# Table seeds by VectorE in 32-bit words, and nine more up products through ScalarE, in a fused S4 convolution and gated GLU

## The chip, the cores and the metric

The kernel runs on one core of a Trainium2 chip. The time is that of one execution in device microseconds; a kernel's time is the median of its runs. The engines are TensorE (PE in the profile, with PEld for its weight loads), VectorE (DVE), ScalarE (ACT), GpSimd (POOL) and SyncE (SP), which here issues most of the DMAs.

## The reference

The input u has 2048 tokens of 512 features. It is layer-normed to xn, and the output is a sum of three terms:

```python
xn = _layernorm(x, axis=-1)
return x + _A_ref(xn, A_re, A_im, B_re, B_im, C_re, C_im, log_dt, Dskip) + _B_ref(xn, w_gate, w_up, w_down)

# _A_ref: a convolution along the tokens, one kernel K per feature, from 128 complex modes
logdA = dt * A ; dB = dt * Bc
P = jnp.exp(logdA[:, :, None] * l[None, None, :])        # l = 0 .. 2047
K = jnp.einsum("dn,dnl,dn->dl", Cc, P, dB).real
y = irfft(rfft(K padded) * rfft(xn padded))[:L] + xn * Dskip
# _B_ref
h = _sigmoid(x @ w_gate) * (x @ w_up)                    # 512 -> 1792
return h @ w_down                                        # 1792 -> 512
```

In the reference the lags l are cast to bfloat16, so that lags above 256 fall on a coarser grid.

## The kernel before, in words

Two jobs share the engines. The GLU goes in four groups of 512 tokens. For each of the 14 tiles of 128 hidden features TensorE computes a gate product (L1045) and an up product (L1069) into PSUM, ScalarE applies the sigmoid to the gate (L1057, or L1060 for two at once), and VectorE multiplies. For the tiles in `UEV` ScalarE first copies the up product from PSUM to a buffer `us_sb` (L1084); two neighbours share a buffer of 2 x 512, and VectorE multiplies both at once on SBUF alone (L1089). The other tiles are multiplied straight from PSUM (L1094). The down products (L1123) follow.

The convolution goes by a transform over blocks of tokens. Its kernel K is built from tables, in four chunks c of 128 features. A ladder of squarings gives the powers W[k] with exponent 2^k (L669 to L678, cast at L661 and L663). From W the kernel builds G (16 lags) and H (41 lags, `LAG0`), each laid out with 64 pairs of features outermost, then real or imaginary, then the lag, then the two features of a pair. H is seeded with eight lags that are entries of W: the copies at L775 to L777, run by ScalarE, or by VectorE for the operation numbers in `ON_DVE` (L288 and L286 in the profile, with the other copies of the helper). The other lags come from complex products (`powers`, L737 to L743) and from squares (`squares`, ScalarE at L791, VectorE at L796 and L797). When a chunk's tables are done, TensorE multiplies G and H (L822, two halves of 64 matmuls for each chunk), ScalarE evicts the results to `kq_sb`, two DMAs store them to `k_scr` (L833, 96 KB each), and a DMA per chunk brings them back in another layout (L837, 192 KB). Two chunks make a half p of the features. A short VectorE operation adds the skip term (L844), and only then the transformed kernel of that half can be computed (L911), evicted, multiplied with the transformed input (L916 and L920), and transformed back (L935). Eight units of work u per half do this. The half swaps that L916 needs are DMAs (L893) or, for five units of the second half, VectorE copies (L898). The results go through memory once more and are summed with the GLU in the tail (L994, L1020, L1143).

The order of work is written out by hand. `_Plan.add` numbers the operations as they are created, `ORDER` lists all the numbers, and `run` issues them in that order; each engine keeps the order of its own operations. The costs, priorities and due times handed to `add` (`PSIG`, `PPROD` and so on) thus have no part in the order of issue. Buffers are pools of slots, taken and given back in the order of the list. To find what stands ahead of what on an engine, one counts off the creations and looks the numbers up in `ORDER`. Some of the numbers for c = 3 and the half that it ends:

| operation | number before | number after |
|---|---|---|
| first and last seed copy | 337 to 344 | 321 to 323 |
| last part of the last powers (L742, L743) | 366 | 345 |
| last part of G | 335 | 319 |
| G times H, first half (L822) | 367 | 346 |
| stores to k_scr | 371, 372 | 350, 351 |
| reload of the half | 277 and 373 in parts | 352 |
| skip term (L844) | 374 | 353 |

Of the kernel before, what the change touches and what calls it, by code (L numbers as in the profile page):

```python
# [10 lines left out]
BF = mybir.dt.bfloat16  # L11
# [14 lines left out]
FT = 14  # L26
# [3 lines left out]
CW = 128  # L30
# [17 lines left out]
FLIP = ((0, 3), (0, 5), (1, 0), (1, 1), (1, 2), (1, 4), (1, 5), (1, 6), (2, 0), (2, 4), (3, 2))  # L48
# [13 lines left out]
LAG0 = [0, 1, 3, 5, 7, 6, 4, 2, 8, 10, 14, 12, 9, 11, 13, 15, 256, 262, 260, 258, 264, 266, 270, 268, 524, 520, 516, 512, 780, 776, 772, 768,  # L62
        1024, 1032, 1544, 1536, 1280, 1288, 1800, 1792, 2048]
EXP = {5: 1, 9: 1, 10: 1, 11: 3, 17: 1, 21: 1, 22: 1, 23: 3, 24: 3, 25: 1, 26: 1, 28: 3, 29: 1, 30: 1, 33: 3, 34: 3, 35: 1, 37: 3, 38: 3, 39: 1}
# [118 lines left out]
def _consts():  # L183
# [19 lines left out]
UEV = (6, 7, 10, 11, 12, 13, 14, 15, 16, 17, 18, 19, 22, 23, 24, 25, 26, 27, 28, 29, 30, 31, 32, 33, 34, 35, 36, 37, 38, 39, 40, 41, 44, 45, 46, 47, 52, 53, 54, 55,)  # L203
ON_DVE = (86, 89, 104, 106, 121, 122, 123, 137, 138, 184, 194, 195, 198, 199, 201,)
ON_ACT = (2,)
ORDER = [
# [112 lines left out]
def kernel(  # L319
# [61 lines left out]
    def at(off, shape, dt=BF):  # L381
# [141 lines left out]
    for n in (0, 5, 6):  # L523
        keep_warm(3 if n < 3 else 1, -9 + n)
# [688 lines left out]
```

## Time and profile before

| | |
|---|---|
| median of 3 runs | 215.45 us (214.41 to 215.57) |
| the profiled execution | 215.32 us, of which its span 213.4 us |
| mean granted TensorE clock | 0.997 |
| PE busy | 204.0 us |
| DVE busy | 191.3 us |
| ACT busy | 176.3 us |
| POOL busy | 33.1 us |
| DMA, mean over the span | 200 GB/s |

The span runs from the first to the last instruction of the profiled execution; its times are measured from its start. In the groups of instructions a line gives the line of the kernel, engine and operation, the output and input by name and form, the count, then the busy time and the mean ns of one, then the idle time of the engine ahead of them. Instructions on one engine overlap a little at their ends, so that the distance from start to start is shorter than the duration. In the rows of busy time by stretch the engines stand in the order PE, PEld, DVE, ACT, POOL, with the granted clock, the share of the DMA engines and GB/s behind them. In a row of waits stand the total in us, the number of waits and the longest.

### The profile page before, as it was taken

What the parts mean: (1) busy time and instruction counts of PE and PEld (TensorE: products, weight loads), DVE (VectorE), ACT (ScalarE), POOL (GpSimd) and SP (SyncE); (2) the same over time, 40 slices, a digit from 0 to 9 for tenths busy, and PEclk for the clock granted to TensorE, in tenths of its full rate; (3) what the DMA queues carried; (4) which work ended last, traced back from release to release, by engine and by line L of the source; (5) the groups of instructions that cost most, each with busy time, mean ns of one, the idle gap of its engine ahead of it and who ended that gap; (6) DMA issues with size and microseconds to landing.
All of it is one profiled execution on the core that took longest, in us unless ns stands there. A gap on an engine that the chain in (4) does not pass through costs nothing.

```text
span 213.4 us, 4897 instructions
## 1 busy us (share of the span) xinstructions
PE 204.0 (96%) x1839; PEld 103.2 (48%) x1864; DVE 191.3 (90%) x406; ACT 176.3 (83%) x284; POOL 33.1 (15%) x40
## 2 busy tenths in 40 slices
PE   7989999999999999999999999999999999999892
PEld 2654444444444454345447464444644655644472
DVE  4799999999999999999999999999973999990494
ACT  4799999999999999998998999779979699960000
POOL 2108030003040000010009970011200000000000
PEclk9999999999999999999999999999999999999998
DMA  5998597013963218788776369589994789897955
GB/s 148 330 372 313 182 225 237 2 52 133 260 139 60 98 55 263 185 238 212 215 216 159 112 174 275 141 231 244 175 257 112 203 252 335 246 288 209 263 195 178
DMA packets 52377, 42.61 MB, mean 200 GB/s; under 512 B 16641, under 2 KB 44546, under 8 KB 52354
## 3 DMA queue, kind: packets, MB, share of 16 engines
q1 hardware_dynamic: 50658, 40.30, 64.3%
q0 software_dynamic: 864, 1.57, 4.8%
q10 hardware_dynamic: 832, 0.43, 0.8%
q8 instruction: 14, 0.23, 0.4%
q14 instruction: 9, 0.07, 0.1%
HBM read 24.99 MB, written 12.85 MB: 177 GB/s over the span
## 4 chain that ended last, share of the span: by engine, by line
PE 59%; ACT 20%; DMA 9%; DVE 6%; issue 4%; POOL 1%; DVEq 0%; ACTq 0%; SPq 0%
PE bank L1069 15%; PE bank L1123 13%; PE bank L1045 11%; PE pair L911 9%; ACT big L288 6%; PE pair L935 5%; ACT hT_sb L1057 3%; PE pair L1045 3%; DMA k_scr<-kq_sb 3%; ACT us_sb L1084 3%; ACT big L669 3%; ACT big L663 2%; DVE big L1020 2%; DMA big<-v_scr 2%; PE pair L822 2%
## 5 line engine op out<-in xcount | busy, mean ns | idle before, releaser
L288 ACT ACTIVATE big<-pair 128x1024 bf16<-128x1024 f32 x64 | 64.6, 1048 | 5.3 <-PE pair L911 2.2
L1069 PE MATMUL bank<-xnT,wu_sb 128*128 128x512 bf16 x212 | 53.0, 379 | 1.1 <-issue 0.6
L1123 PE MATMUL bank<-wd_sb,hT_sb 128*128 128x512 bf16 (+1 forms) x231 | 50.6, 367 | 0.5 <-issue 0.2
L1045 PE MATMUL bank<-xnT,wg_sb 128*128 128x512 bf16 (+1 forms) x194 | 46.6, 370 | 0.5 <-issue 0.3
L1045 PEld LDWEIGHTS <-wg_sb 128*128 128x128 bf16 x240 | 22.7, 98 | 25.8 <-issue 3.0
L1123 PEld LDWEIGHTS <-hT_sb 128*128 128x128 bf16 x238 | 22.4, 98 | 24.9 <-issue 1.9
L1069 PEld LDWEIGHTS <-wu_sb 128*128 128x128 bf16 x224 | 20.7, 98 | 25.5 <-issue 3.4
L1057 ACT ACTIVATE hT_sb<-bank 128x512 bf16<-128x512 f32 x48 | 28.7, 640 | 2.3 <-PE bank L1045 2.3
L737 DVE TENSOR_TENSOR big<-big 128x1024 bf16<-128x1024 bf16 (+4 forms) x40 | 26.8, 670 | 0.2
L738 DVE TENSOR_TENSOR big<-big 128x1024 bf16<-128x1024 bf16 (+4 forms) x40 | 26.6, 666 | 0.0
L1084 ACT ACTIVATE us_sb<-bank 128x512 bf16<-128x512 f32 x40 | 24.7, 640 | 0.0
L911 PE MATMUL pair<-big 128*128 128x256 bf16 x160 | 19.4, 273 | 0.4 <-DVE big L844 0.4
L916 DVE TENSOR_TENSOR big<-big 128x2048 bf16<-128x2048 bf16 x16 | 19.3, 1219 | 0.1
L846 POOL COPY hold<-big 1x1 bf16<-1x1 bf16 x2 | 14.3, 7146 | 30.7 <-DVE big L844 30.7
L911 PEld LDWEIGHTS <-big 128*128 128x128 bf16 x160 | 15.3, 98 | 4.8 <-issue 1.0
L742 DVE TENSOR_TENSOR big<-big 128x512 bf16<-128x512 bf16 (+4 forms) x40 | 16.6, 415 | 0.3
L743 DVE TENSOR_TENSOR big<-big 128x512 bf16<-128x512 bf16 (+4 forms) x40 | 16.6, 414 | 0.0
L791 ACT ACTIVATE sq_sb<-big 128x256 bf16<-128x256 bf16 (+2 forms) x20 | 14.0, 698 | 1.3 <-DVE big L743 1.0
L935 PE MATMUL pair<-big 64*64 64x512 bf16 (+1 forms) x256 | 13.1, 327 | 0.5 <-ACT big L288 0.3
L1089 DVE TENSOR_TENSOR hT_sb<-hT_sb,us_sb 128x1024 bf16<-128x1024 bf16 x20 | 13.5, 684 | 0.0
L288 ACT ACTIVATE big<-big 128x256 bf16<-128x256 bf16 x30 | 13.1, 463 | 0.0
L669 ACT ACTIVATE big<-big 128x1024 f32<-128x1024 f32 x11 | 12.4, 1125 | 0.4 <-DVE big L678 0.4
(100 smaller groups left out, 233.4 us busy)
## 6 DMA issues: line engine op xcount, KB each, us to landing
big<-c_E SPq DMA_DIRECT2D x13, 320.0 KB, 5.1
z_scr<-big SPq DMA_DIRECT2D x16, 256.0 KB, 3.0
big<-z_scr SPq DMA_DIRECT2D x16, 256.0 KB, 3.9
v_scr<-big SPq DMA_DIRECT2D x16, 256.0 KB, 4.1
big<-big SPq DMA_DIRECT2D x44, 64.0 KB, 3.3
big<-in_A_u_dram SPq DMA_DIRECT2D x4, 512.0 KB, 6.7
wu_sb<-in_B_w_up_dram SPq DMA_DIRECT2D x2, 896.0 KB, 10.6
wd_sb<-in_B_w_down_dram SPq DMA_DIRECT2D x1, 1792.0 KB, 8.3
```

What stands on the lines that cost most here:

```text
L288: nc.scalar.activation(out=get(out), in_=get(in_), func=ACT.Identity)
L669: s_op = pl.add("ACT", 0.95, lambda cur=cur, sq=sq: S.activation(out=sq, in_=cur, func=ACT.Square), [cur_op] + W_op[-1:], PLAD + k * 0.01)
L737: V.tensor_tensor(out=wide(outp), in0=wide(lo), in1=mre, op=ALU.mult)
L738: V.tensor_tensor(out=wide(tb()), in0=wide(lo), in1=mim, op=ALU.mult)
L911: T.matmul(two(sk)[:, o:o + DW], es()[:, g, kt, :], kTv[p][:, :, kt, :], start=kt in (0, NKT - 1), stop=kt >= NKT - 2)
L916: V.tensor_tensor(out=pp().rearrange("p q h m -> p (q h) m"), in0=xx().rearrange("p q h m -> p (q h) m"), in1=kb()[:, 0:2 * DW].unsqueeze( ...
L935: T.matmul(two(sv)[o:o + 64, DW * (2 * g + y):2 * DW * (g + 1)], mab[b:b + 64, 2 * u + g, q, :], pq()[b:b + 64, q, ch] if y else pp()[b:b ...
L1045: T.matmul(bank(sl, k % 2)[:, c0:c1], w[:, kt, k * 128:(k + 1) * 128], xnT[:, grp, kt, c0:c1], start=(kt == 0), stop=(kt == KT - 1))
L1057: S.activation(out=hT_sb[:, hs.idx, k % 2, :], in_=bank(sl), func=ACT.Sigmoid)
L1069: T.matmul(bank(sl), wu_sb[:, kt, k * 128:(k + 1) * 128], xnT[:, grp, kt, :], start=(kt == 0), stop=(kt == KT - 1))
L1084: eus.append(pl.add("ACT", 0.48, lambda sl=sl, us=us, kk=kk: S.activation(out=us_sb[:, us.idx, kk % 2, :], in_=bank(sl), func=ACT.Identity ...
L1123: T.matmul(bank(po)[:, 0:c[1] - c[0]], hT_sb[:, hts[k // 2].idx, k % 2, jj * 128:(jj + 1) * 128], wd_sb[:, k, c[0]:c[1]], start=first and ...
```

## The change

The seed copies are taken out of the helper and given to VectorE. Two features of a pair, 4 bytes, are moved as one 32-bit word, and several seeds go in one copy: 1, 3, 2 and 2 of them in four copies for c = 0, and 1, 3 and 4 in three copies for each other chunk, 13 copies for the 32 seeds. For that the lags of H are put in another order, the entries of W in another order of slots (`WS`), and the squares and products that fill H follow. The constant matrices built from `LAG0` and `EXP` on the host follow too.

Forty-nine up products in place of 40 are copied by ScalarE. Each has a buffer of its own (two buffers of 512), and each is multiplied by itself; the joint product of two neighbours and `FLIP` are gone.

The reload of the kernel is one DMA of 384 KB per half (before, two of 192 KB), and all the stores are issued by SP (before, one of the last two by ScalarE). Rows 2 and 3 of the input come in one load. The warm-up matmuls at the start are 14 and 3 + 3 + 1 + 1 (before, 12 and 3 + 1 + 1). The scratch that the program keeps for dynamic DMAs goes back to its default. `ORDER` is new as a whole.

```diff
-LAG0 = [0, 1, 3, 5, 7, 6, 4, 2, 8, 10, 14, 12, 9, 11, 13, 15, 256, 262, 260, 258, 264, 266, 270, 268, 524, 520, 516, 512, 780, 776, 772, 768,
-        1024, 1032, 1544, 1536, 1280, 1288, 1800, 1792, 2048]
+LAG0 = [0, 1, 3, 5, 7, 8, 2, 4, 6, 10, 14, 12, 9, 11, 13, 15, 256, 264, 258, 260, 262, 266, 270, 268, 512, 516, 520, 524,
+        768, 772, 776, 780, 1024, 1032, 1536, 1544, 1280, 1288, 1792, 1800, 2048]
+WS = (0, 2, 3, 1, 4, 5, 6, 7, 8, 9, 10, 11)
...
-    us_sb = const.tile([128, 2, 2, 512], BF, name="us_sb")
+    us_sb = const.tile([128, 2, 512], BF, name="us_sb")
...
+    def words(nm, n):
+        return big[:, OFF[nm] // 2:OFF[nm] // 2 + 2 * n].bitcast(I32)
...
-    load_x(2, 1)
-    load_x(3, 1)
+    load_x(2, 2)
...
-    keep_warm(12, -10)
-    for n in (0, 5, 6):
+    keep_warm(14, -10)
+    for n in (0, 1, 5, 6):
...
-        for dst, src in ((1, 0), (7, 1), (6, 2), (8, 3), (16, 8), (27, 9), (32, 10), (40, 11)):
-            seeds[dst] = pl.copy(nc, 0.31, H[:, :, :, dst, :].rearrange("p r c h -> p c r h"),
-                                 W[c // 2][:, src, :, ws].rearrange("p c (r h) -> p c r h", h=2), [W_op[src], w0_op, qb] + hdep, PC)
+        H32 = words("H", 2 * NPR * NH).rearrange("p (r c k) -> p k c r", c=2, k=NH)
+        W32 = words("W%d" % (c // 2), 12 * DW).rearrange("p (s c d) -> p s c d", s=12, c=2)[:, :, :, CW // 2 * (c % 2):][:, :, :, 0:CW // 2]
+        for dst, src, step in ((1, (0,), 1), (5, (3, 1, 2), 1)) + (((16, (8, 9), 8), (32, (10, 11), 8)) if c == 0 else ((16, (8, 9, 10, 11), 8),)):
+            n = len(src)
+
+            def f_seed(dst=dst, s0=WS[src[0]], n=n, step=step, H32=H32, W32=W32):
+                V.tensor_copy(out=H32[:, dst:dst + step * (n - 1) + 1:step], in_=W32[:, s0:s0 + n])
+            o_seed = pl.add("DVE", 0.15 + 0.12 * n, f_seed, [W_op[x] for x in src] + [w0_op, qb] + hdep, PC)
...
-        squares(5, 2, 1, ["2"])
         powers(3, 1, 2, 2, [1, "2"])
         powers(12, 1, 4, 3, [1, "2", "3"])
-        squares(9, 3, 3, ["3", "5"])
-        powers(17, 5, 7, 8, [6, 7, 8, "5", "9"])
-        squares(24, 17, 3, ["17"])
-        powers(28, 24, 4, 8, [27, "24"])
-        squares(33, 26, 1, ["24"])
-        squares(34, 30, 2, ["28"])
+        squares(8, 2, 3, ["2", "3"])
+        squares(11, 8, 1, ["8"])
+        powers(17, 5, 7, 8, [5, 6, 7, "8", "11"])
+        squares(25, 18, 3, ["17"])
+        powers(28, 24, 4, 8, [24, "25"])
+        squares(33, 25, 1, ["25"])
+        squares(34, 28, 2, ["28"])
...
-        kq_free = [dma("ACT" if cc and c in (3,) else "SP", k_scr[4 * c:4 * c + 4, :, :, cc, :].rearrange("t i h x -> (t i) h x"),
+        kq_free = [dma("SP", k_scr[4 * c:4 * c + 4, :, :, cc, :].rearrange("t i h x -> (t i) h x"),
...
-        k_ld.append(dma("SP", kT[pc][:, half_kT].rearrange("p a c k y -> p a (c k y)"), k_scr[4 * c:4 * c + 4].rearrange("a i h c x -> (i h) a (c x)"),
-                        deps=kq_free + W_op + [o_g], prio=PC, pkt=384)(192 * KB))
         if c % 2 == 0:
             continue
+        kr = dma("SP", kT[pc].rearrange("p a c k y -> p a (c k y)"), k_scr[8 * pc:8 * pc + 8].rearrange("a i h c x -> (i h) a (c x)"),
+                 deps=k_st[pc] + W_op + [o_g], prio=PC, pkt=384)(384 * KB)
...
-                    def fpd2(hs=hs, us=us):
-                        hh = hT_sb[:, hs.idx, :, :].rearrange("p k n -> p (k n)")
-                        V.tensor_tensor(out=hh, in0=hh, in1=us_sb[:, us.idx, :, :].rearrange("p k n -> p (k n)"), op=ALU.mult)
...
+                def fpd(sl=b, h=h, us=us, on=on):
+                    V.tensor_tensor(out=h(), in0=h(), in1=us_sb[:, us.idx, :] if on else bank(sl), op=ALU.mult)
...
-    nc = _bacc.Bacc("TRN2", target_bir_lowering=False, num_devices=1, dynamic_dma_scratch_size=8192)
+    nc = _bacc.Bacc("TRN2", target_bir_lowering=False, num_devices=1)
```

More of the change, by code (lines that the diff above doesn't have):

```diff
@@ L660, in f_cast @@
             if dve:
-                V.tensor_copy(out=W[p][:, k], in_=cur[:, :, DW * p:DW * p + DW])
+                V.tensor_copy(out=W[p][:, WS[k]], in_=cur[:, :, DW * p:DW * p + DW])
             else:
-                S.activation(out=W[p][:, k], in_=cur[:, :, DW * p:DW * p + DW], func=ACT.Identity)
+                S.activation(out=W[p][:, WS[k]], in_=cur[:, :, DW * p:DW * p + DW], func=ACT.Identity)
     cast_prev = [None, None]
@@ L720 @@
     kT_op = [[], []]
-    k_ld = []
     k_st = [[], []]
@@ L774 @@
         seeds = {}
-        for dst, src in ((1, 0), (7, 1), (6, 2), (8, 3), (16, 8), (27, 9), (32, 10), (40, 11)):
-            seeds[dst] = pl.copy(nc, 0.31, H[:, :, :, dst, :].rearrange("p r c h -> p c r h"),
-                                 W[c // 2][:, src, :, ws].rearrange("p c (r h) -> p c r h", h=2), [W_op[src], w0_op, qb] + hdep, PC)
+        H32 = words("H", 2 * NPR * NH).rearrange("p (r c k) -> p k c r", c=2, k=NH)
[5 more added lines that the diff above has]
+            o_seed = pl.add("DVE", 0.15 + 0.12 * n, f_seed, [W_op[x] for x in src] + [w0_op, qb] + hdep, PC)
+            for m in range(n):
+                seeds[dst + step * m] = o_seed
         h_ops = {}
@@ L1075, with feu @@
                 un = FT * grp + k
+                us = _Slot("us")
                 on = un in UEV
[L1078 to L1095 removed]
+                def feu(sl=b, us=us, on=on):
+                    if on:
+                        S.activation(out=us_sb[:, us.idx, :], in_=bank(sl), func=ACT.Identity)
+                eu = pl.add("ACT", 0.48, feu, [mu], PSIG, acq=[us] if on else [], rel=[b] if on else [], alt=(un, 1))
+                def fpd(sl=b, h=h, us=us, on=on):
+                    V.tensor_tensor(out=h(), in0=h(), in1=us_sb[:, us.idx, :] if on else bank(sl), op=ALU.mult)
+                tail = dict(rel=[us] if on else [b], alt=(un, 2))
                 if joint and k % 2 == 0:
[L1097 removed]
+                    held = fpd, [eu, mu], tail
                     continue
@@ L1100 @@
                     prods.append(pl.add("DVE", 0.33, held[0], held[1] + [es_], PPROD, **held[2]))
-                prods.append(pl.add("DVE", 0.33, fpd, [es_, mu], PPROD, **tail))
+                prods.append(pl.add("DVE", 0.33, fpd, [es_, eu, mu], PPROD, **tail))
         ges = []
```

26 lines of the change are left out of this document (5 added, 21 removed), and 81 rows, old and new, of the table ORDER.

## The prediction

> **What bounds the kernel now.** I read the page first, then busy time by stretches, then who waits for whom on TensorE and VectorE, then the timeline where the last table ends, then groups by form for prices.
>
> ```profile
> span 213.4 us, 4897 instructions
> PE 204.0 (96%) x1839; PEld 103.2 (48%) x1864; DVE 191.3 (90%) x406; ACT 176.3 (83%) x284; POOL 33.1 (15%) x40
> ```
>
> ```profile
> 14.00:80.00 66.00, 65.59 (x454) 29.19 (x460) 65.71 (x156) 65.57 (x110) 11.66 (x18) 1.00 0.53 153
> 80.00:154.00 74.00, 73.15 (x720) 36.92 (x729) 73.47 (x160) 68.43 (x119) 18.64 (x11) 1.00 0.76 202
> 154.00:165.50 11.50, 10.83 (x207) 5.25 (x208) 6.45 (x11) 10.17 (x14) 0.00 (x0) 1.00 0.73 188
> 165.50:192.40 26.90, 26.15 (x261) 15.02 (x266) 26.45 (x46) 22.58 (x28) 0.43 (x1) 1.00 0.90 266
> ```
>
> The page puts TensorE first (96%) and VectorE second (90%). The stretches (PE, PEld, DVE, ACT, POOL) show that VectorE's 90% is no average of half-busy stages: from 14 to 154 us it works 139.2 of 140.0 us, from 165.5 to 192.4 us 26.45 of 26.9, and between the two lies its one hole in the middle. TensorE is as full. Neither has slack ahead of 154 us, and the waits say so too:
>
> ```profile
> PE pair L1045 <- DVE xnT L574: 0.8, 1, 0.8
> PE bank L1069 <- issue: 0.6, 4, 0.2
> PE pair L994 <- DMA big<-v_scr: 0.5, 1, 0.5
> PE pair L911 <- DVE big L844: 0.4, 1, 0.4
> PE pair L935 <- ACT big L288: 0.3, 1, 0.3
> PE bank L1045 <- issue: 0.3, 2, 0.2
> PE bank L1123 <- issue: 0.2, 1, 0.2
> ```
>
> ```profile
> DVE big L1020 <- PE pair L994: 6.6, 1, 6.6
> DVE big L898 <- issue: 4.4, 1, 4.4
> DVE big L844 <- DMA big<-k_scr: 0.5, 1, 0.5
> ```
>
> All that a better order could win back on TensorE behind its start (where L1045 waits for the first features) is 0.6 + 0.5 + 0.4 + 0.3 + 0.3 + 0.2 = 2.3 us. VectorE waits 6.6 us in the tail and 4.9 us around 160 us, where the last table travels through memory. What decides is how the two meet at the last table:
>
> ```profile
> 153.18 0.43 DVE L742 TENSOR_TENSOR big<-big 128x512 bf16<-128x512 bf16 x1
> 153.52 0.43 DVE L743 TENSOR_TENSOR big<-big 128x512 bf16<-128x512 bf16 x1
> 154.03 1.53 PE L822 MATMUL pair<-big 128*32 128x82 bf16 x128
> ```
>
> VectorE ends the last powers at 153.95 and TensorE starts the matmuls on them (L822, c = 3) at 154.03. So VectorE's queue up to there sets when the last table starts. From there on a fixed chain follows, seen in the chain of work that ended last:
>
> ```profile
> 155.73 0.81 ACT kq_sb L288
> 156.56 6.16 DMA k_scr<-kq_sb
> 162.74 2.72 DMA big<-k_scr
> 165.49 0.29 DVE big L844
> ```
>
> Behind L844 VectorE is full again until 192.4 us (26.45 of 26.9), with the products of the second half that the end needs. So each microsecond by which VectorE comes later to the last table, or by which the store and reload take longer, moves the end by about as much, whatever TensorE could do.
>
> **The change part by part.** Durations first; the last number ahead of the idle time is the mean ns of one.
>
> ```profile
> L288 ACT ACTIVATE big<-big 128x256 bf16<-128x256 bf16 x30 | 13.1, 463 | 0.0
> L1084 ACT ACTIVATE us_sb<-bank 128x512 bf16<-128x512 f32 x40 | 24.7, 640 | 0.0
> L661 DVE CAST big<-big 128x512 bf16<-128x512 f32 x4 | 1.5, 420 | 0.0
> L286 DVE COPY big<-big 128x256 bf16<-128x256 bf16 x6 | 1.7, 281 | 0.0
> ```
>
> ```profile
> 31.85 0.26 DVE L286 COPY big<-big 128x256 bf16<-128x256 bf16 x1
> 31.98 0.68 DVE L1094 TENSOR_TENSOR hT_sb<-hT_sb,bank 128x512 bf16<-128x512 bf16 x1
> ...
> 189.28 1.29 DVE L1089 TENSOR_TENSOR hT_sb<-hT_sb,us_sb 128x1024 bf16<-128x1024 bf16 x2
> ...
> 190.48 1.88 DVE L1094 TENSOR_TENSOR hT_sb<-hT_sb,bank 128x512 bf16<-128x512 bf16 x3
> ```
>
> On a full engine an instruction costs its start-to-start distance, which is less than its duration: 0.13 us for a seed copy (31.85 to 31.98), 1.29 − 0.68 = 0.61 for a wide product, (1.88 − 0.68) / 2 = 0.60 for one that reads a bank, and 0.34 for a 128x512 operation on SBUF alone (153.18 to 153.52), which is the form that a narrow product takes after the change.
>
> *ScalarE.* Its 30 copies of this form are 27 of the 32 seeds (ON_DVE names the other five) and three first columns of G; the 27 go, and nine up copies come: −27 × 0.463 + 9 × 0.640 = −12.5 + 5.8 = −6.7 us busy. I take nothing from it for the end: what waits for ScalarE on TensorE is 0.3 us. Each up copy now takes one of two single buffers and waits for the product two before it, with the PSUM evictions queued behind. With VectorE full this can only lose; I take 0, as the fixed order leaves products close behind their copies, and keep up to 1 us.
>
> *Seeds on VectorE.* Thirteen copies carry the 32 seeds as 128 words each, in place of five copies that cost 5 × 0.13 = 0.65 us. The trace shows no 32-bit copy of this layout. The nearest row moves the same 128 words, in pieces of one word, to the same places in H: L286, 0.13 us. So 32 × 0.13 = 4.2 us with nothing for the start of an instruction; with 0.28 − 0.13 = 0.15 us for each start, 13 × 0.15 more, 6.1 us. The far row on the other side is L661: 512 four-byte elements in 0.42 us, contiguous, or (0.42 − 0.15) / 512 × 128 = 0.07 us a seed, so 32 × 0.07 + 13 × 0.06 = 3.0 us. I take 4.6, near the row with the same places; net +3.9.
>
> [...]
>
> *Products.* Counted in the two orders, ahead of the last table operation stand 16 wide products and 10 from a bank before, and 35 narrow and 7 from a bank after: 16 × 0.61 + 10 × 0.60 = 15.8 against 35 × 0.34 + 7 × 0.60 = 16.1 us, +0.3. All else ahead of it is the same: as many power and square operations of the same sizes, six pairs of L916 and L920, the ladder and the layernorm.
>
> *Head.* The new order fills VectorE's early idle time with two more feature statistics and with L610.
>
> ```profile
> 7.55 0.17 DVE L493 RECIPROCAL ln_ri_f<-ln_sd_b 128x2 f32<-128x2 bf16 x1 [0.75 <-POOL ln_sd_b L492]
> ...
> 9.94 0.43 DVE L618 TENSOR_SCALAR big<-big 128x512 f32<-128x512 f32 x1 [0.25 <-ACT big L615]
> ```
>
> That is 0.75 + 0.25 = 1.0 us of gaps; I take −0.9 (0 to −1.2). The x rows 2 and 3 in one load save one issue, and the five warm-up matmuls more run while TensorE waits for its input anyway; both at 0, since L1045 waits for VectorE's L574 there (0.8 us).
>
> So the last table starts 3.9 + 0.3 − 0.9 = 3.3 us later, at about 157.3.
>
> *Store and reload.* Both last stores go on SP's queue, one issue (0.6 us) later for the second. The reload is one of 384 KB per half instead of two of 192 KB, and in the second half stands ahead of SP's eight half-swap copies (L893) that before had four ahead of it; they need be there only when L916 follows, about 2.3 us behind the reload's L844.
>
> ```profile
> big<-k_scr SPq DMA_DIRECT2D x4, 192.0 KB, 5.0
> ...
> k_scr<-kq_sb SPq DMA_DIRECT2D x7, 96.0 KB, 3.3
> ```
>
> The store of 6.16 us is long against its median of 3.3: it meets z loads and swaps that are then in flight. Coming 3.3 us later it meets fewer; I take 4.3 (3.3 to 6.2). The reload took 2.72 for half the bytes (median 5.0): I take 2.72 + 1.2 = 3.9 (3.4, with 192 KB more at 266 GB/s, to 5.0 + 0.7 = 5.7). Together 0.7 less, between 2.2 less and 3.0 more. The first half's reload has cover, seen in the timeline as the issue of its last part and the first L911:
>
> ```profile
> 106.12 0.36 SPq L422 DMA_DIRECT2D big<-k_scr  x1
> ...
> 112.42 1.26 PE L911 MATMUL pair<-big 128*128 128x256 bf16 x10
> ```
>
> 106.12 plus 2.7 to 5.0 us leaves 1.3 to 3.6 us of cover; if that is gone, it costs what it lacks.
>
> Sum: 3.3 − 0.7 = +2.6 on a span of 213.4; the rest of the profiled execution (215.32, close to the median of 215.45) lies outside the span and stays. That gives 217.9.
>
> **The rivals.** *Seeds at the contiguous price.* [...] The seeds then cost 3.0 and not 4.6: −1.6, so 216.3, within 0.5%. L661 speaks for it, L286 against. [...]
>
> *ScalarE's relief decides: faster.* The chain of work runs through ScalarE from 36.4 to 78.8 us; its first and last pieces there:
>
> ```profile
> 36.44 0.65 ACT us_sb L1084
> ...
> 76.86 1.95 ACT big L288 x2
> ```
>
> So the tables might be late by ScalarE's squares and casts, with VectorE full only because it is given its other work early. Then 6.7 us less on ScalarE bring the tables to TensorE in time, and its 2.3 us of waits go: 215.3 − 2.3 = 213.0. It decides if VectorE's work ahead of the last table can end before 153.95 in spite of 3.9 us more for seeds, that is if VectorE now has hidden idle time of over 3 us. Its 139.2 busy of 140.0 us speaks against.
>
> *The reload stays long.* The store takes its 6.16 again and the reload the 5.7 of its bound: 3.7 us more than in the sum, 221.6. For: it queues behind two z loads of 256 KB that the order puts between store and reload. Against: those are issued while SP waits for the store.
>
> **How the numbers follow.** The main case gets 0.56, the cheap seeds 0.17, ScalarE's relief 0.12, the long reload 0.15. The main case alone spans 215.7 (seeds 4.2, head −1.2, store and reload −2.2) to 220.3 (seeds 6.1, head 0). About 0.5%, 1.1 us, is what a measurement can tell from no change: 214.4 to 216.5 is the same. Faster: the relief's 0.12. Same: 0.10 of the cheap seeds and 0.05 of the main case, 0.15. Slower: the rest, 0.73. For 8 in 10 the range takes in the main case, the cheap seeds and the nearer half of the long reload, 214.5 to 221.2; the relief and the rest of the reload, under 0.2, stay outside.
>
> **What would show it.** Right: VectorE without idle time ahead of the last L822, which starts near 157 and not 154; 32-bit copies of about 0.13 us a seed beyond their start; TensorE waiting some 2 to 4 us more, for VectorE at L822 or L911; ScalarE's busy time down by some 6 us with no gain. Wrong step by step: the copies near 0.07 us a seed (price), the last L822 at or before 154 (VectorE had slack), L844 more than 12 us behind it (reload). The forecast is wrong altogether if VectorE shows idle gaps ahead of the last table and the end still moves.

## The result and the profile after

The changed kernel takes 223.68 us (median of 4 runs, 222.2 to 225.94) against 215.12 us before (median of 4). One of the four runs (225.94) fell in a slower state of the chip, so the ratio goes by the other three: 1.038, 95% interval 1.031 to 1.044. The forecast was 217.9. The profiled execution took 223.99 us, span 222.1. The page after:

```profile
span 222.1 us, 4926 instructions
PE 209.1 (94%) x1869; PEld 104.3 (47%) x1869; DVE 194.7 (88%) x434; ACT 174.1 (78%) x266; POOL 51.5 (23%) x40
```

VectorE got 3.4 us more to do (the forecast had 4.2 ahead of the last table) and ScalarE 2.2 less, where the forecast had 6.7. That forecast was a sum of durations, and by durations ScalarE did fall by 6.1 (30 seed and first-column copies of 463 ns to 3 of 483, 40 up copies of 640 ns to 49 of 652). But neighbours on one engine overlap (the durations of all of ScalarE's instructions add up to 213.7 us before and 204.7 after, for 176.3 and 174.1 busy), so its busy time fell by about a third of that. POOL was no part of the forecast, and its busy time went from 33.1 to 51.5 us.

The starts of the four tables cut both executions into three parts: up to the first table, from there to the last, and to the end. TensorE's timeline, before (where the third table comes in two halves) and after:

```profile
77.98 1.67 PE L822 MATMUL pair<-big 128*32 128x82 bf16 x128
98.73 1.42 PE L822 MATMUL pair<-big 128*32 128x82 bf16 x128
127.30 0.80 PE L822 MATMUL pair<-big 128*32 128x82 bf16 x64
129.34 0.80 PE L822 MATMUL pair<-big 128*32 128x82 bf16 x64
154.03 1.53 PE L822 MATMUL pair<-big 128*32 128x82 bf16 x128
```

```profile
80.59 1.86 PE L831 MATMUL pair<-big 128*32 128x82 bf16 x128 [2.89 <-POOL big L773]
104.52 1.42 PE L831 MATMUL pair<-big 128*32 128x82 bf16 x128
132.03 1.45 PE L831 MATMUL pair<-big 128*32 128x82 bf16 x128
161.59 1.42 PE L831 MATMUL pair<-big 128*32 128x82 bf16 x128
```

| us | up to the first table | first to last table | from the last table to the end | span |
|---|---|---|---|---|
| before | 78.0 | 76.05 | 59.4 | 213.4 |
| after | 80.6 | 81.0 | 60.5 | 222.1 |

So 2.6 us come ahead of the first table, 5.0 between the tables and 1.1 behind the last one. The last table starts 7.6 us late, not 3.3.

The first part is told by the wait in the first row: TensorE stood 2.9 us at L831 for POOL's memset L773. GpSimd's timeline ahead of that matmul (rows are left out at the dots):

```profile
56.39 1.08 POOL L1159 DMA_DIRECT2D glu_sb<-in_A_u_dram  x1 [13.16 <-ACT glu_sb L289]
57.15 21.84 POOL L712 CAST pre<-xnT 128x4 f32<-128x4 bf16 x1
79.08 0.91 POOL L714 TENSOR_TENSOR pre<-pre,xnT 128x4 f32<-128x4 f32 x3
...
80.32 0.21 POOL L773 MEMSET big<- 128x128 bf16 x1
```

L712 is the first copy of the small prefix sums `f_pre`, four elements per partition. Before, it took 0.39 us at 17.60 (L709 there). The new order puts it behind the first accumulating DMA (L1159), which waits for ScalarE, and ahead of the memsets of H. It stood there for 21.84 us, and the memsets behind it. VectorE's timeline shows what that does next:

```profile
78.26 0.67 DVE L740 TENSOR_TENSOR big<-big 128x1024 bf16<-128x1024 bf16 x1
78.92 0.42 DVE L1093 TENSOR_TENSOR hT_sb<-hT_sb,us_sb 128x512 bf16<-128x512 bf16 x1
82.49 0.52 DVE L783 COPY big<-big 128x128 int32<-128x128 int32 x1 [3.15 <-PE pair L831]
```

The next table's first seed overwrites H, so it waits until L831 has read it: 3.15 us of idle VectorE, where there were none before. The chain of work puts 10% of the span on this one copy.

The second part is a full TensorE. Busy time by stretch, after (PE, PEld, DVE, ACT, POOL, then the clock, the share of the DMA engines and GB/s):

```profile
14.00:80.60 66.60, 63.08 (x330) 27.45 (x329) 64.96 (x160) 66.53 (x109) 28.51 (x15) 1.00 0.52 157
80.60:161.60 81.00, 81.00 (x879) 40.59 (x878) 78.39 (x179) 62.65 (x94) 19.78 (x14) 0.98 0.69 178
161.60:173.90 12.30, 10.48 (x205) 4.80 (x204) 7.00 (x14) 11.59 (x17) 0.45 (x1) 1.00 0.85 200
```

and the same stretch, first to last table, of before:

```profile
77.98:154.03 76.05, 75.10 (x852) 38.47 (x862) 75.45 (x163) 70.48 (x122) 18.90 (x12) 1.00 0.74 197
```

TensorE has 81.00 us of 81.00, VectorE has slack. Its weight loads went from 862 to 878. The orders say what the 16 are: 38 gate and up blocks of four matmuls stand between the two tables, in place of 34. Ahead of the first table there are three fewer, behind the last one there is one fewer. Four blocks of four matmuls, 0.216 us each from start to start, are 3.45 us. The granted clock of 0.98 in this execution accounts, by estimate, for another 1.3 or so (81.0 against 79.7 us in e7 at a granted clock of 1.00, below).

Last, store and reload, in the chain of work after:

```profile
164.61 5.01 DMA k_scr<-kq_sb
169.62 0.02 SPq L426
169.65 0.03 issue
169.68 4.16 DMA big<-k_scr
```

From L831 to L852 it is 173.86 − 161.59 = 12.3 us, 11.5 before. The last store starts 3.0 us behind the table (164.61 − 161.59), 2.5 before (156.56 − 154.03): both stores are now issued one behind the other by SP.

### The profile page after: what moved, and what is told of

The parts are those of the page before. It is cut to its first block, busy times and chain, and to the rows that moved or that the text cites. A ratio compares the mean times of both kernels' runs of the same rounds, so it can differ in the third digit from the quotient of the medians.

```text
span 222.1 us, 4926 instructions
## 1 busy us (share of the span) xinstructions
PE 209.1 (94%) x1869; PEld 104.3 (47%) x1869; DVE 194.7 (88%) x434; ACT 174.1 (78%) x266; POOL 51.5 (23%) x40
## 4 chain that ended last, share of the span: by engine, by line
PE 44%; DVE 23%; POOL 11%; DMA 11%; ACT 5%; issue 2%; SPq 2%; DVEq 0%; ACTq 0%
PE bank L1122 11%; POOL pre L712 10%; PE bank L1053 9%; PE bank L1077 9%; PE pair L919 7%; PE pair L943 4%; DVE hT_sb L1093 3%; DVE stats L545 3%; DMA big<-v_scr 3%; DVE big L613 3%; PE pair L831 2%; DMA k_scr<-kq_sb 2%; DMA big<-in_A_par_dram 2%; DVE big L681 2%; SPq L426 2%
## 5 line engine op out<-in xcount | busy, mean ns | idle before, releaser
L1077 PE MATMUL bank<-xnT,wu_sb 128*128 128x512 bf16 x224 | 55.9, 386 | 0.1
L1053 PE MATMUL bank<-xnT,wg_sb 128*128 128x512 bf16 (+1 forms) x200 | 47.7, 371 | 1.1 <-ACT xnT L575 0.6
L1077 PEld LDWEIGHTS <-wu_sb 128*128 128x128 bf16 x224 | 21.4, 99 | 26.7 <-issue 4.6
L1089 ACT ACTIVATE us_sb<-bank 128x512 bf16<-128x512 f32 x49 | 30.6, 652 | 3.8 <-DVE hT_sb L1093 1.9
L740 DVE TENSOR_TENSOR big<-big 128x1024 bf16<-128x1024 bf16 (+4 forms) x40 | 26.4, 660 | 0.0
L1093 DVE TENSOR_TENSOR hT_sb<-hT_sb,us_sb 128x512 bf16<-128x512 bf16 x49 | 19.7, 414 | 3.2 <-ACT us_sb L1089 2.1
L712 POOL CAST pre<-xnT 128x4 f32<-128x4 bf16 x1 | 21.8, 21845 | 0.0
L854 POOL COPY hold<-big 1x1 bf16<-1x1 bf16 x2 | 15.0, 7518 | 24.5 <-DVE big L852 24.5
L924 DVE TENSOR_TENSOR big<-big 128x2048 bf16<-128x2048 bf16 x16 | 19.3, 1216 | 0.4 <-ACT big L289 0.4
L800 ACT ACTIVATE sq_sb<-big 128x768 bf16<-128x768 bf16 (+2 forms) x20 | 13.6, 678 | 6.3 <-DVE big L745 5.7
L545 DVE BATCH_NORM_STATS2 stats<-big 128x6 f32<-128x512 bf16 x15 | 9.9, 679 | 3.8 <-DMA big<-in_A_u_dram 3.8
```

The lines of the kernel that those rows point to most:

```text
L712: P.tensor_copy(out=pre[:, :, 0], in_=xnT[:, 0, :, 0])
L740: V.tensor_tensor(out=wide(tb()), in0=wide(lo), in1=mim, op=ALU.mult)
L1053: T.matmul(bank(sl, k % 2)[:, c0:c1], w[:, kt, k * 128:(k + 1) * 128], xnT[:, grp, kt, c0:c1], start=(kt == 0), stop=(kt == KT - 1))
L1077: T.matmul(bank(sl), wu_sb[:, kt, k * 128:(k + 1) * 128], xnT[:, grp, kt, :], start=(kt == 0), stop=(kt == KT - 1))
L1089: S.activation(out=us_sb[:, us.idx, :], in_=bank(sl), func=ACT.Identity)
L1093: V.tensor_tensor(out=h(), in0=h(), in1=us_sb[:, us.idx, :] if on else bank(sl), op=ALU.mult)
```

## The experiments

Two theories for the 5.8 us that the forecast lacks. *GpSimd's queue*: the late prefix sums hold the memsets, these the table, the table VectorE. *VectorE's queue alone*: the wait takes the place of others that would come anyway, and the excess is the seeds' price and the rest of the forecast's terms. Each run was timed in rounds with the kernel before; the ratio is to that. Where `ORDER` was changed the lines stand one to three higher.

**The prefix sums back to their old place.**

```
ORDER: 183 (f_pre) moved to right behind 100 (GpSimd's roots of the second layernorm group)
```

> The changed kernel with one thing undone: GpSimd's prefix sums (L712 to L716) stand right behind the second layernorm group's reciprocal roots in GpSimd's queue, as in the kernel before, and no longer ahead of the first table's memsets (L773/774). Theory (the late prefix sums hold the memsets, these the first table's matmuls L831, these the next seeds on VectorE, which then idles 3.1 us): the copy takes under 1 us, the memsets are done before 60, L831 of the first table starts at about 77.6 in place of 80.6, VectorE's 3.1 us wait at L783 shrinks to under 0.5, and the kernel takes 223.7 - 3.0 = about 220.7 us (219.9 to 221.5). Rival (what VectorE loses there it would lose anyway, to TensorE's backlog or to waits further on): the row changes but the time stays within 222.7 to 224.7.

219.58 us, ratio 1.022 (1.019 to 1.025): 4.1 us won by the medians, 3.4 by the ratios (1.038 to 1.022). GpSimd's timeline and TensorE's first and last table:

```profile
20.78 0.39 POOL L713 CAST pre<-xnT 128x4 f32<-128x4 bf16 x1
...
57.27 0.53 POOL L774 MEMSET big<- 128x128 bf16 x1
57.42 0.52 POOL L775 MEMSET big<- 128x128 bf16 x1
```

```profile
77.72 1.44 PE L832 MATMUL pair<-big 128*32 128x82 bf16 x128
...
157.92 1.42 PE L832 MATMUL pair<-big 128*32 128x82 bf16 x128
```

The first table starts at 77.7, VectorE's wait is gone. That GpSimd's queue held the first table, and that this costs 3 to 4 us, is shown.

**The same sums, still late, but behind the memsets.**

```
ORDER: 183 moved to right behind 193 (the first table's memsets)
```

> The changed kernel with the prefix sums still late in GpSimd's queue, but behind the first table's memsets in place of ahead of them. If the wait of the memsets in GpSimd's queue is the whole cost, the copy L712 still takes over 18 us, to near 79, and the time is that of the early prefix sums, 219.6 us (218.8 to 220.4). If a starved GpSimd instruction costs something by itself (slower VectorE or DMAs), the time stays above 221.

219.26 us, ratio 1.022 (1.018 to 1.026), and the copy is as slow as ever:

```profile
56.71 0.57 POOL L774 MEMSET big<- 128x128 bf16 x1
56.86 0.56 POOL L775 MEMSET big<- 128x128 bf16 x1
57.01 21.55 POOL L713 CAST pre<-xnT 128x4 f32<-128x4 bf16 x1
```

So a GpSimd instruction of 21 us costs nothing by itself here. What stands behind it costs.

**What holds the copy.** Three runs: the accumulating DMA put behind it, the copies written as another operation, and the late place put into the kernel before.

```
e2: ORDER: 666 (accumulating DMA) moved to right behind 193 (memsets)
e3: -P.tensor_copy(out=pre[:, :, 0], in_=xnT[:, 0, :, 0])
    +P.tensor_scalar(out=pre[:, :, 0], in0=xnT[:, 0, :, 0], scalar1=1.0, scalar2=0.0, op0=ALU.mult, op1=ALU.add)
    (and pre2 likewise)
e4: the kernel before, ORDER: 183 moved to right behind 676 (its accumulating DMA)
```

> The changed kernel with GpSimd's accumulating DMA (L1159 at 56.39) put behind the prefix sums and the memsets, so that no DMA stands just ahead of the copy L712. If the copy's 21.8 us are the work of that DMA (descriptors written by the same engine): L712 under 1 us, the memsets by 60, and about 220.7 us. If the copy is kept out by VectorE's unbroken stream of instructions: L712 still takes over 18 us and ends at VectorE's first gap, near 79, and the time stays at 222.7 to 224.7.

220.60 us, ratio 1.026 (1.022 to 1.031). The run tells less than meant: without the DMA's wait for ScalarE ahead of it the copy ran at 42.80, in 0.26 us, in another stretch of VectorE's work. The additions behind it took 3.63 us for three.

> The changed kernel with the two copies of the prefix sums (L712, L715) written as a multiplication by 1 and an addition of 0 on the same engine, in the same place; the values are the same. GpSimd's multiplication by a table of constants and its power at 42.19 took 0.41 and 1.04 us beside a busy VectorE. If GpSimd's copy as an operation is what starves: the new L712 under 1.5 us, the first table at 77.6, about 220.7 us. If any GpSimd instruction that reads SBUF waits for a gap in VectorE's stream there: over 18 us again, 222.7 to 224.7.

223.27 us, ratio 1.040 (1.037 to 1.044). The multiplication took 21.47 us at 57.57. It is not the copy as an operation.

> The kernel before with the prefix sums moved late in GpSimd's queue, behind the first accumulating DMA and ahead of the first table's memsets: this one part of the change alone. VectorE's stream in that trace has gaps of 0.02 to 0.04 us at 62.04 and 66.74 and none from there to 79.63. If the copy waits for a gap in VectorE's stream: it starts near 60.6 and ends near 62 or 67, ahead of the first table's 78.0, and the time stays at 214.4 to 215.8; if a gap that short is not enough it ends near 79.6, the first table comes 2 us late and VectorE's seeds are not in the way (ScalarE has them), so 215 to 217. If the DMA ahead of it is what holds it: it takes 15 us or more whatever the gaps.

214.90 us, ratio 1.0005 (0.9986 to 1.0024). The copy stands directly behind the DMA, and took 1.49 us. GpSimd's and VectorE's timelines in this run:

```profile
59.49 1.08 POOL L1162 DMA_DIRECT2D glu_sb<-in_A_u_dram  x1 [7.82 <-ACT glu_sb L290]
60.25 1.49 POOL L711 CAST pre<-xnT 128x4 f32<-128x4 bf16 x1
```

```profile
61.61 0.17 DVE L503 RECIPROCAL ln_ri_f<-ln_sd_b 128x4 f32<-128x4 bf16 x1
61.81 0.16 DVE L504 SCALAR_TENSOR_TENSOR ln_nb_f<-ln_m_f,ln_ri_f 128x4 f32<-128x4 f32 x1
```

It ended at 61.74, beside an instruction with one input (L503) that follows three operations with two inputs in SBUF (59.94 to 61.07), and 0.04 us ahead of a gap of 0.03 us. So the DMA alone is out. In the changed kernel the same copy ended at 78.99, just behind the one place since its start where two neighbours, L740 and L1093, follow each other without their usual overlap (L740 ends at 78.93 and L1093 starts at 78.92 in the rows above, 0.01 us, where all the others from 57.15 on overlap by 0.07 or more). In e8 and e3 it ended just behind such a place too (at 78.56 and 79.04, with overlaps of 0.00 and 0.04 us). The late place is harmless in the kernel before: 1.5 us, with nothing waiting. In the changed kernel it met a VectorE stream without a gap (57.15 to 79.34); that the stream is what holds the copy is an estimate read from where it ends, no run opened a gap in it.

**The seeds.** With the sums early there are still 4.9 us against the kernel before. Groups by form, after, for the seeds:

```profile
L783 DVE COPY big<-big 128x384 int32<-128x384 int32 x4 | 3.4, 839 | 0.0
L783 DVE COPY big<-big 128x512 int32<-128x512 int32 x3 | 1.9, 634 | 0.0
```

Three seeds take longer than four. From start to start it is 0.68 us for three, 0.46 for four, 0.22 for two and 0.135 for one; all 13 hold VectorE for 5.1 us (4 × 0.135 + 2 × 0.22 + 4 × 0.68 + 3 × 0.46). Three runs change the price: three split into two and one, all seeds on ScalarE, and the seeds of the first table alone.

```
e5: -V.tensor_copy(out=H32[:, dst:dst + step * (n - 1) + 1:step], in_=W32[:, s0:s0 + n])
    +for a, b in ((0, 2), (2, 3)) if n == 3 else ((0, n),):
    +    V.tensor_copy(out=H32[:, dst + step * a:dst + step * (b - 1) + 1:step], in_=W32[:, s0 + a:s0 + b])
e6: S.activation(out=H[:, :, :, dst + step * m, :]..., in_=W[c // 2][:, s0 + m, :, ws]..., func=ACT.Identity) for m in range(n), on "ACT"
e7: if c == 0: V.tensor_copy(...)
(all with f_pre early, as in the first run)
```

> The changed kernel with the prefix sums early (as in the first run, 219.58 us) and each copy of three seeds split into one of two and one of one, on VectorE in the same place. In the trace of after, a copy of one seed holds VectorE 0.135 us, of two 0.224, of four 0.456, but of three 0.679. If the odd count is what makes it dear, 2 + 1 takes 0.36 in place of 0.68: 4 times 0.32 = 1.3 us less in VectorE's queue. Theory (that queue sets the end): 218.3 us (217.6 to 219.0). Rival (the seeds' price is not on the path): within 0.5 of 219.6.

218.84 us, ratio 1.019 (1.014 to 1.023); two and one now take 0.35 us. The 0.7 won is not outside the intervals.

> The changed kernel with the prefix sums early and all 32 seeds as copies on ScalarE, one by one in 16-bit elements, at the same places of the order; the rest of the change stays. VectorE loses 4.6 us of work ahead of the last table; ScalarE gets 32 copies of 0.46 us, 15 us by durations, where before it had 27. Theory (VectorE's queue sets the end, ScalarE has slack): 219.6 - 4.6 = 215.0, up to 1.5 more for waits on ScalarE, so 215 to 216.5. Rival (the nine more up copies have taken ScalarE's slack, and the single buffers chain it to VectorE): 218 or more, with VectorE waiting for ScalarE's seeds.

226.50 us, ratio 1.056 (1.051 to 1.060): the rival. VectorE's waits in this run:

```profile
DVE hT_sb L1096 <- ACT us_sb L1092: 6.2, 7, 1.7
DVE big L808 <- ACT sq_sb L803: 4.1, 6, 1.2
```

With nine more up copies and single buffers ScalarE has no room for 32 copies at these places: it is busy 90% or more in every slice of the page from 11 us to the first table, as in e5 without these copies (182.3 us in all here, 173.2 in e5), and VectorE waits for its up copies and squares.

> The changed kernel with the prefix sums early and the seeds copied for the first of the four tables alone; the later tables are made from the first one's seeds, so this leaves out part of the computation. It takes 3 x (0.135 + 0.679 + 0.456) = 3.8 us off VectorE's queue and puts nothing elsewhere. Theory: 219.6 - 3.8 = 215.8 us (215.0 to 216.6). Rival (part of the seeds' time is covered by waits that would come anyway): 217 to 219.6.

218.47 us, ratio 1.018 (1.014 to 1.022). VectorE lost 3.8 us of work by the prices above, and the time fell by 1.1 us against e1, which is not outside the intervals. So the theory of VectorE's queue alone falls here. The stretch from the first to the last table in this run:

```profile
77.35:157.00 79.65, 79.57 (x880) 40.12 (x879) 77.24 (x174) 65.25 (x100) 19.14 (x12) 1.00 0.70 191
```

TensorE has 79.57 of 79.65 us, VectorE 2.4 us of slack, and the distance is nearly what it was with all seeds (79.8 in e5, 80.2 in e1 with the seeds undivided). From the second table to the third it is 27.50 to 27.51 us after, in e1, e3, e5 and e7 alike, whatever the seeds cost. How TensorE comes to the last table shows in its rows and VectorE's last one, in this run and then in the kernel before:

```profile
156.00 0.68 DVE L746 TENSOR_TENSOR big<-big 128x1024 bf16<-128x1024 bf16 x1
156.03 1.03 PE L1079 MATMUL bank<-xnT,wu_sb 128*128 128x512 bf16 x4
156.99 1.42 PE L833 MATMUL pair<-big 128*32 128x82 bf16 x128
```

```profile
153.07 1.03 PE L1069 MATMUL bank<-xnT,wu_sb 128*128 128x512 bf16 x4
154.03 1.53 PE L822 MATMUL pair<-big 128*32 128x82 bf16 x128
```

VectorE ends at 156.68, and TensorE starts the table at 156.99, when the up block ahead of it is through, 0.96 us from start to start. In e1 it is 0.96 too (156.96 and 157.92), and in the kernel before (153.07 and 154.03). So TensorE's own work holds the last table in e7, and before it was there at the same moment as VectorE, not waiting for it.

**Is it TensorE's start?** In the changed kernel and its variants TensorE starts the first features' matmul at 9.7 to 10.2 us, before at 8.55. ScalarE copies the features behind a step of the table's angles, five more warm-up matmuls stand there, and the first gate weights land later (at 9.64 in e9, at 8.27 before). Four runs put these back by and by, e10 and e13 with the first table's seeds alone; two put one thing each into the kernel before; one moves the last table's first matmuls ahead of an up block.

```
e9:  e5 + ORDER: 50 behind 35 (feature copy first on ScalarE); the added warm-up of 3 matmuls left out
e10: e7 + the same
e12: e9 + ORDER: 15 (1 KB load) behind 14; 24 and 26 (row statistics) exchanged
e13: e7 + the same as e12
e14: e12 + ORDER: 346 (L831, first half, c = 3) moved to right behind 319
e11: the kernel before, ORDER: 49, 50 moved to right behind 48 (angle step ahead of the feature copy on ScalarE)
e15: the kernel before, ORDER: 16 (1 KB load) moved ahead of the first gate weights
```

> The kernel of e5_early_2_1 (prefix sums early, seeds two and one; 218.84 us) with the start put right: ScalarE copies the first features to SBUF (L576, 8.64 us there, 7.47 in the kernel before) ahead of the step L619 of the table's angles, which waits 0.8 us for VectorE, and the three added warm-up matmuls that stand behind the first transposes are left out. TensorE's first features' matmul then starts near 8.6 in place of 9.7. Theory (behind the start TensorE is full and sets the end together with VectorE; in e5 VectorE ended the last table's operations at 156.59 and TensorE was ready for it at 156.89): part of the 1.1 us is won, 0.3 to 1.1, so 217.7 to 218.5. Rival (VectorE's queue alone sets the end): 218.5 or more.

219.32 us, ratio 1.024 (1.020 to 1.027): nothing won. TensorE now waited for the gate weights until 9.68.

> The same start as e9_head, with the seeds copied for the first table alone (as in e7_early_seeds_once, 218.47 us; part of the computation is left out). If TensorE's late start is what holds that kernel (its TensorE has no gap from 77 to 157 us), the 1.1 us come in full: 217.3 us (216.6 to 218.0). If something else holds it: 218 or more.

218.91 us, ratio 1.022 (1.019 to 1.025): nothing won.

> The kernel before with one change at the start: on ScalarE the step L615 of the table's angles (waits for VectorE's L610) stands ahead of the copy of the first features L572, as in the changed kernel. VectorE's and TensorE's orders stay. The copy comes at 9.9 in place of 7.47, so TensorE's first features' matmul at about 10.9 in place of 8.55, 2.4 us late. If TensorE has no slack behind its start: 214.6 + 2.4 = 217.0 us (216.2 to 217.6). If VectorE's queue alone sets the last table, as the prediction had it: 214.6, at most 0.5 more.

215.86 us, ratio 1.005 (1.002 to 1.009). TensorE's first gate matmul started at 10.75, 2.2 us late; the first table came 0.9 late (78.88), and all behind it too. So the start has over a microsecond of slack, and counts beyond.

> The kernel of e9_head (219.32 us) with two more things put as in the kernel before: the 1 KB load of the skip vector stands behind the large loads in SP's queue and no longer ahead of the first gate weights, and VectorE takes the statistics of row 0 ahead of those of row 1. In e9_head the first gate matmul waited for those weights until 9.68 (they landed at 9.64; in the kernel before at 8.27). If the small load ahead of them is what delays them: they land by 8.5, TensorE's first features' matmul starts at 8.5 to 8.8, and the time falls by 0.3 to 1.1 against 218.84 of e5_early_2_1, to 217.7 to 218.5. If VectorE's queue alone sets the end from there: 218.5 to 219.3 though the start is earlier.

219.15 us, ratio 1.022 (1.019 to 1.025). TensorE waited 1.61 us for the weights all the same, until 9.91. The small load is not all that delays them.

> The same start as e12_full_head with the seeds copied for the first table alone (part of the computation is left out). VectorE then has work to spare, and TensorE's start is that of the kernel before. If the late start was what held e7_early_seeds_once (218.47 us): 217.3 us (216.6 to 217.8). If the rest comes from the order of TensorE's work (one more block of 0.86 us ahead of the last table): 217.8 or more.

219.42 us, ratio 1.024 (1.020 to 1.028).

> e12_full_head with the last table's first matmuls (L831's) moved ahead of the last up block in TensorE's order, directly behind VectorE's last operation on that table. In e5_early_2_1 VectorE ended at 156.59 and the table started at 156.89. If TensorE's order holds the table: it starts 0.3 to 0.9 us earlier and the time falls by as much against e12_full_head. If VectorE holds it: TensorE waits there for VectorE, 0 to 0.3 won.

219.74 us, ratio 1.024 (1.021 to 1.027). The first four matmuls of the last table started at 156.08, then TensorE waited 0.38 us for VectorE's L746 and went on at 156.68. Without the up block ahead of it TensorE is thus ready 0.4 us before VectorE. But the second half stayed behind the up block, at 158.34 against 157.5: the move was half done, and won nothing.

> The kernel before with one change: the 1 KB load of the skip vector stands ahead of the first gate weights in SP's queue, as in the changed kernel. If that small load delays them: they land at 8.7 to 9.7 in place of 8.27, and the first gate matmul starts up to 1.1 us later than 8.55; with 1 us of slack at TensorE's later wait for L574, the time grows by 0 to 0.5 us (214.6 to 215.1). If it does not: landing at 8.3 and no change.

214.85 us, ratio 1.002 (1.000 to 1.004). TensorE waited 1.79 us for the weights, the first gate matmul started at 9.94, 1.4 us late, and the end hardly felt it. Whether the small load delayed them is not settled by one trace: in e12 and e14, whose starts are the same, that matmul starts at 9.91 and 8.66.

The start is thus not the cause of what is left. In e9, e10, e12 and e13 the first table starts at 77.5 to 77.8, and the last one 79.7 us behind it.

**TensorE's work taken away.** Eight up blocks ahead of the first table sum over half of their rows: 16 matmuls, 3.45 us.

```
-for kt in range(KT):
+ks = range(2 if grp == 1 and k < 8 else KT)
+for kt in ks:
```

> The kernel of e5_early_2_1 (prefix sums early, seeds two and one; 218.84 us) with 16 matmuls fewer on TensorE ahead of the first table: eight up blocks of the second token group sum over half of their rows, so part of the computation is left out. That is 16 x 0.216 = 3.45 us of TensorE's work; VectorE's and ScalarE's work stays. If TensorE's work ahead of the last table holds this kernel alone, about 215.4 us. If VectorE's queue holds it as well (it ended the last table at 156.59, TensorE was ready at 156.89): 0.3 to 1 won, 217.8 to 218.5.

218.46 us, ratio 1.018 (1.016 to 1.021).

> The kernel of e7_early_seeds_once (seeds for the first table alone, 218.47 us) with the same 16 matmuls left out; both leave out part of the computation. If TensorE holds e7: VectorE's queue without waits would end the last table 2.5 us ahead of e5's 156.59, at 154.1, TensorE 3.45 us ahead of 156.99, at 153.5; so 2.9 us won, 215.6 us (215.0 to 216.5). If something else holds e7 (DMAs, ScalarE): over 217.

218.42 us, ratio 1.019 (1.016 to 1.022). No gain clear of noise in either. The matmuls were taken from the wrong stretch: the first table starts at 77.7 (77.1 in e5) and 76.6 (77.4 in e7), and the distance to the last grows to 80.4. The first up block behind the first table waits 0.39 us there for ScalarE's up copy, and from that block to the last table it is 78.3 to 78.4 us in e5, e7, e16 and e17 alike. Up to the first table something else than TensorE sets the pace; behind it, the blocks that are still there.

> The kernel before with the same 16 matmuls left out (part of the computation is left out). The prediction's premise was that VectorE's queue sets the last table there (154.03), with TensorE full but not the bound: then 0 to 0.7 us won, 213.8 to 214.5. If TensorE's order is the bound there, up to 3.4 us: 211.1.

217.89 us, ratio 1.016 (1.012 to 1.020), slower with less work. TensorE's timeline around the last table in this run:

```profile
153.86 1.42 PE L822 MATMUL pair<-big 128*32 128x82 bf16 x128
155.21 0.61 PE L1045 MATMUL bank<-xnT,wg_sb 128*128 128x512 bf16 x2
158.75 0.60 PE L1045 MATMUL bank<-xnT,wg_sb 128*128 128x512 bf16 x2 [2.93 <-issue]
```

The first and the last table start where they did (77.84, 153.86), so TensorE's work ahead of the first table was not the bound before either. The loss comes behind: within one gate block TensorE stands 2.9 us at a matmul ahead of which the profile shows nothing that it waits for. What it waits for stays open; one packet of the instruction queue (0.02 MB between 156 and 157 us) lies in that stretch, but that it is the cause is not shown. So the run does not tell what less work on TensorE would be worth.

## Why the prediction was wrong

The direction was right; the time came out 5.8 us over the forecast and 2.5 over the range.

*Where it failed.* The step is the sentence "All else ahead of it is the same", with "Counted in the two orders" ahead of it. It is true of VectorE's queue, whose counts hold. But only VectorE's order was counted, and two other queues had changed. GpSimd's was put at nothing without a reason, and it is 3.4 to 4.1 us of the 5.8. TensorE's makes "whatever TensorE could do" wrong: with the seeds of three tables left out the last table still starts 3.0 us late (156.99 for 154.03).

*GpSimd's queue.* The number of `f_pre` stands at another place of `ORDER`. That term was missing altogether: 4.1 us by the medians of e1 and 4.4 by those of e8, 3.4 and 3.5 by the ratios. The forecast named as its own refutation that "VectorE shows idle gaps ahead of the last table", and it did: 3.15 us at L783.

*What is left.* The profiled run of e1 (219.81) is 1.9 us over the forecast. The last table is 0.6 late (157.92 for 157.3), from there to the skip term it takes 0.9 more than forecast (11.7 for 11.5 − 0.7 = 10.8), and the rest, 0.4, comes behind the reload and outside the span.

*TensorE's queue.* Four blocks more between first and last table make that stretch 79.7 us and not 76.05, also with the seeds of three tables left out (e7). The prediction had VectorE's queue set the last table, from its end at 153.95 and TensorE's start at 154.03. But none of the waits that it shows is one of TensorE at L822, and the up block ahead was through at 154.03 too. In the changed kernel both queues are late by about as much: VectorE ended at 157.82 in e1, with the table at 157.92, and TensorE comes at 157.0 with most of the seeds gone (e7). So of the 3.9 us by which the table is late in e1, VectorE's seeds add 0.9 to what TensorE's order gives anyway. This is worked out from the traces and the orders; no run took a block out of that stretch.

*VectorE's sum* came close, 157.82 against 157.3, in part by luck. By distances from start to start in e1 the seeds came to 4.4 us net for 3.9, the products to +0.4 for +0.3, and the idle time fell by 0.1 for 0.9. The 307 other instructions, as many in both kernels, came out 1.0 us shorter in sum, which no term foresaw.

*The seeds' price.* 4.6 forecast, 5.1 measured, and spread otherwise than at one price a seed: 0.88 to 1.06 ns per word with one, two and four seeds, 1.77 with three. Why three cost more no run shows; as two and one they took 0.35 us in place of 0.68 (e5). No run shows the rival's rate for words that lie apart, 0.07 us a seed; the copies took 0.11 to 0.14 us a seed with one, two and four, and 0.23 with three. The rival of the cheap seeds is out.

*Products.* 0.34 us each from start to start, as priced, in the trace of e1; +0.4 in sum for +0.3.

*Head, −0.9.* Mostly not won. The two gaps are gone, but VectorE waits longer for the first input (3.8 us in place of 3.1; 2.9 in e14 to 3.6 in e8). Up to 14 us it is busy 9.76 us in place of 9.70, and about 10.1 in e5.

*Store and reload, −0.7.* Mis-sized: 12.3 us from L831 to L852 after, 11.7 in e1, 11.5 before, so +0.2 to +0.8. The prediction's own sign of a wrong reload, more than 12 us, came after and not in e1. The two transfers took 5.01 and 4.16 us after, for 4.3 and 3.9 forecast. And "one issue (0.6 us) later for the second" is named in the prediction and not added in its sum, and the last store does start 0.5 us later behind the table (3.0 for 2.5).

*ScalarE's relief* is out as a rival: no variant that has it is faster than the kernel before. But the nine more up copies have used it up: with the seeds returned to ScalarE (e6) the kernel takes 7 us more than with them on VectorE.

*The premise*, that the chain from the last table to the end is fixed, held to about a microsecond: 58.4 to 60.8 us in the changed kernel and its variants, 59.4 before. The exception is e14 (61.9), where the table starts early in halves.

No run beat the kernel before. The best variant of the changed kernel that computes everything is e5, at 1.019.

## What to carry to other kernels

Where the order of work is written out, compare the queue of every engine up to the point that sets the end, the idle GpSimd too: one four-element copy at another place of its queue cost 3.4 to 4.1 us, and leaving out the seeds of three tables won back 1.1. In these runs a slow instruction on an idle engine was free until something that was needed stood behind it (21.55 us in e8, at 219.26 us for 219.58 with the copy early; 21.84 us ahead of the memsets, at 223.68), so put such work behind what others wait for. And if two engines are both full at the critical point, price a change for both: relieving or loading one of them moves the end only as far as the other lets it (in e7 3.8 us less on VectorE moved it by 1.1).

## What the runs showed of the hardware

- A GpSimd instruction on four elements that reads SBUF stood 21.5 to 21.8 us (a copy in the changed kernel and in e8, a multiplication in e3), and a copy of one element 13.9 us (the kernel before) to 19.3 us (e2), while VectorE was busy; a memset, which reads nothing, took 0.2 to 0.6 us (0.53 at 57.27 in e1, beside the same stream). In e4 the copy took 1.49 us and ended beside an instruction with one input (L503, 61.61); but in the changed kernel casts and copies with one input (63.10 and 67.74), some fifty VectorE instructions in all (57.15 to 78.99), ran while the copy stood. It does not always happen: in the changed kernel GpSimd's power took 1.04 us at 42.19 and in e2 a copy 0.26 at 42.80, beside a busy VectorE. What decides is open.
- In the changed kernel the 32-bit copies of the seeds into H cost 1.77 ns per word from start to start with three seeds and 0.89 with four. In e5 two copies (two and one) take 0.35 us, where the one of three takes 0.68.
- The first gate weights landed at 8.27 us in the kernel before and at 9.64 in e9, after nearly the same issue (3.54 in the kernel before, 3.43 in e5, whose loads e9 keeps), with no clear cause. Between e12 and e14, whose starts are the same, the first matmul on them differs by 1.25 us (9.91 and 8.66), so that one trace each cannot tell what a 1 KB load ahead of them costs (that matmul starts at 8.55 without and 9.94 with it in the kernel before).
- In e18, with sixteen matmuls fewer, TensorE stood 2.9 us at a place where the profile shows nothing that it waits for, and the kernel was 3.4 us slower. In e16 and e17, with the same matmuls left out of the other kernel, it stood at no such place.
